# A recurrent attention with routed experts on Trainium2: score tile AB in two halves, two reads of a bank declared independent, capacity made a float elsewhere

## The chip, the cores and the metric

The kernel runs on one core of one Trainium2 chip. The metric is the device time of one execution in microseconds (us). A core has five engines with their own instruction queues: PE (TensorE, matrix products), DVE (VectorE), ACT (ScalarE), POOL (GpSimd) and SP (SyncE, which here only issues DMAs). They work side by side and wait for one another through semaphores. Matrix products are summed in banks of a memory of its own (PSUM, 128 partitions), from which ACT and DVE read. Tiles lie in SBUF, also over 128 partitions.

## The reference

Three stages follow one another. The first is a linear recurrence per batch and head (4 x 8 of them, 768 tokens, width 40):

```python
for t in range(S):
    y[:, :, t] = einsum('bhd,bhde->bhe', r_t, state)
    Sa = einsum('bhde,bhe->bhd', state, a_t)
    state = state * w_t[:, :, None, :] - einsum('bhd,bhe->bhde', Sa, b_t) + einsum('bhd,bhe->bhde', v_t, k_t)
```

Its output, 3072 tokens of width 320, is routed: each token goes to the expert with the largest logit, as the next row of that expert, as long as the expert has fewer than `capacity` rows (768, an input of the kernel). Each of the 8 experts computes `relu(x @ w1) @ w2` on its rows, times the gate. A last dense layer with ELU between two products (320 to 2048 to 320) runs on all 3072 tokens.

## The kernel before

**Attention** (`attention`, L76 to L673). The recurrence is computed in chunks of 64 tokens. A unit u (0 to 23) is one chunk of 16 of the 32 sequences, in two parts g. The order of all steps is written by hand, in the string `ORDER` (L33): a letter, the unit and the part, so `c8.1` is the next piece of the scores of unit 8, part 1. What follows is the order of instructions on each engine; no scheduler moves anything, and each engine goes through its own queue in order.

- `scores` (c, L229): four products on PE fill a PSUM bank "sc". ACT copies partitions 64 to 127 of it to the tile AB (L238). After part 1, SP sends AB to memory, as dab (L245, L248). There is one AB, in partitions 64 to 127, for all units: the copy of a unit waits until the DMA of the unit before has read it.
- `am_evac` (m, L250): DVE multiplies partitions 0 to 63 of the same bank by the mask and writes AM (L252). The framework takes the two reads of a bank, L238 and L252, as ordered: the second in the program waits for the first.
- `lm_load` (l, L287) loads dab back, row by row, for `solve` (i, L299 to L310), a triangular solve on POOL for a group of 2 or 4 units (`GROUPS`). Its result X goes out (dx, L316), and comes back as TT and TA (L336 to L342).
- `t64` (g, L379) puts the 64x64 inverse together from 32x32 blocks: DVE transposes a block of TA into T11 (L383), PE multiplies (xp, L390). T11 lies in the first 32 partitions of AB, which the scores don't use.
- `u_solve` (L426, L428), `vu_tr` (L436, L440), `s_update` (st, L451), `q_mm`, `y_mm` (Qs L487, y L509) carry the state on and make the output y, in RVU, VU, Qs, KB.
- `route` and `route_mm` (L526 to L564) choose the expert of each token and its row (roh, ACC, SLOT); `scatter` (L567) sends the rows to `disp`. `first` (F, L597) writes some index tiles on POOL, and `hot` (H, L583 to L593) prepares the first tokens of the experts with a one-hot product, pt.

**Experts and dense layer** (`ffn`). Weights are fetched by SP (L802, L804), split into a high part by ACT (L776) and a low part by POOL (L781). `marks` (L1259) runs first: on DVE it turns the capacity, an integer of two words (CAP), into a float (cf, four instructions L1262 to L1265); on POOL it sets some constants. Then `prep` (L944): ACT writes XH, the high part of the turned tokens (L953), DVE the rest, XL (L954), and `s1` (L969) multiplies the high and low weights by XH, then the high ones by XL, then both by XS (the last 64 rows). H and L (L1099, L1100) are the high and low parts of the hidden layer, po the second product (L1034 to L1042).

The lines of the attention and of `marks` that are touched:

Of the kernel before, what the change touches and what calls it, by code (L numbers as in the profile page):

```python
# [22 lines left out]
SL = 448  # L23
# [3 lines left out]
NU = 24  # L27
LOOK = 9

FU, KMU = 4, 8  # L30
GROUPS = [(u, 2) for u in range(0, FU, 2)] + [(u, 4) for u in range(FU, NU, 4)]

ORDER = """  # L33
# [42 lines left out]
def attention(tc, nc, e_in, v_tok, d_in, wg, disp, xt, cst, ring, early, early_w, cv, cap, after):  # L76
    ident, mask = cst["ident"], cst["mask"]
# [12 lines left out]
    sh = [ring.tile(i, F32) for i in (0, 1, 3)]  # L90
# [29 lines left out]
    XTs = [two.tile([128, 4, 128], F32, name="XT")]  # L120
    SD = [two.tile([128, 344], F32, name=f"SD{i}") for i in range(2)]
    AB = two.tile([128, 2, 4, 128], F32, name="AB")
    T11 = AB[:, 0].rearrange("p j (h t) -> p (j h) t", t=32).rearrange("p (b h) t -> p b h t", b=2)
    IW = two.tile([128, 4, 88], F32, name="IW")
    gap = two.tile([128, 1], F32, name="gap")
    st = {}
# [99 lines left out]
    def by_row(m):  # L226
        return m[:, 0:4096].rearrange("l (s t) -> s l t", t=64)

    def scores(u, g):  # L229
        A, kb = Abd[u % 2], KBt[u % 2]  # L230
        p = st["sc", u, g] = bank("sc")
        for i in range(4):
            q = 4 * g + i
            nc.tensor.matmul(  # L234
                p[:, 128 * i:128 * i + 128], kb[:, q].rearrange("p x t -> p (x t)"),
                A[:, :, q, :], start=True, stop=True)
        yield
        nc.scalar.copy(AB[64:128, :, 2 * g:2 * g + 2], p[64:128, :].rearrange("p (j b y) -> p b j y", j=2, b=2))  # L238
        if g == 0:
            return  # L240
        yield
        src = AB[64:128].rearrange("s b j (x t) -> s (b j x) t", t=64)
        if u < FU:
            st["dab", u] = dab = dr.tile([16, 4160], F32, name=f"dab{u}")
            nc.sync.dma_start(out=by_row(dab), in_=src)  # L245
        else:
            st["dab", u] = dab = dr.tile([64, 16, 64], F32, name=f"dab{u}")
            nc.sync.dma_start(out=dab, in_=src)  # L248

    def am_evac(u, g):  # L250
        AM, p = AMs[u % (LOOK + 1)], st["sc", u, g]
        nc.vector.tensor_tensor(  # L252
            AM[0:64, 4 * g:4 * g + 4].rearrange("p q x t -> p (q x) t"), p[0:64, :].rearrange("p (l t) -> p l t", t=64),
            mask[0:64].unsqueeze(1).to_broadcast([64, 8, 64]), op=ALU.mult)

    def kb_tr(u, g):
        kb, K = KBt[u % 2], KB[u % NKB]
# [121 lines left out]
    def t64(u):  # L379

        T, TA, TB = TT[u % 2], st["TA", u], TBs[u == 1]
        if u >= FU:
            nc.vector.transpose(out=T11[0:32].rearrange("p b h t -> p (b h t)"), in_=TA[64:96].rearrange("p b h t -> p (b h t)"))  # L383
            yield
        p = bank("xp")
        for h in range(8):
            for bp in range(2):
                r = slice(64 * bp, 64 * bp + 32)
                m, x = (st["M", u][r, h, 32:64], TB[r, h, 0]) if u < FU else (TA[0:32, bp, h], T11[0:32, bp, h])
                nc.tensor.matmul(p[64 * bp + 32:64 * bp + 64, 32 * h:32 * h + 32], m, x, start=True, stop=True)  # L390
# [223 lines left out]
    def warm(n):  # L614
        w = early_w.B[0]
        p = bank("warm")
        for _ in range(n):
# [4 lines left out]
                 b=route, j=route_mm, D=scatter, H=hot, F=first, W=lambda n, k: warm(n), Z=zero_d, X=zero_x, V=lambda: cv.pieces(spare, CVN))  # L622
# [60 lines left out]
def consts(p):  # L683

    c = {}
    c["ident"] = p.tile([128, 128], F32, name="ident")
    c["mask"] = p.tile([128, 64], F32, name="mask")
    for nm in ("ones", "tri"):
        c[nm] = p.tile([128, 128], BF, name=nm)
    c["desc"] = p.tile([128, 8], F32, name="desc")  # L690
    c["ebase"] = p.tile([128, 8], F32, name="ebase")
    c["lg"] = p.tile([128, 24, 9], F32, name="LG")
    c["oh"] = p.tile([128, 2, 8, 12], BF, name="OH")
    c["slot"] = p.tile([128, 24], I32, name="SLOT")
    c["acc"] = p.tile([128, 2, 8], BF, name="ACC")
    c["cap"] = p.tile([128, 2], I32, name="CAP")
    c["x"] = p.tile([128, 2048], F32, name="X0")
    c["xo"] = c["x"][:, 1536:1536 + RW]
    c["row"] = c["x"][:, 1536 + RW:1648 + RW]
    c["off"] = c["x"][:, 1648 + RW:1652 + RW]  # L700
    return c
# [185 lines left out]
def ffn(tc, nc, cst, disp, xt, w1, w2, w32, out, ring, W0, cv, ps, turned):  # L887
# [228 lines left out]
    def gates():  # L1116
# [3 lines left out]
        for nm in ("blk", "tmo", "l1"):  # L1120
# [19 lines left out]
        t = T("t", [128, 2, 8, 12])  # L1140
        nc.vector.tensor_tensor(t, p1.rearrange("p (b e c) -> p b e c", b=2, e=8),
                                b.unsqueeze(3).to_broadcast([128, 2, 8, 12]), op=ALU.add)
        nc.vector.scalar_tensor_tensor(out=t, in0=t, scalar=over["cap"], in1=OH, op0=ALU.is_lt, op1=ALU.mult)
        kp = T("kp", [128, 24])
        nc.vector.tensor_reduce(kp.rearrange("p (c b) -> p b c", b=2), t.rearrange("p b e c -> p b c e"), axis=AX.X, op=ALU.add)
        eb0 = T("eb0", [128, 8])
# [111 lines left out]

    def marks():  # L1259

        cw, cf = cst["cap"], ap.tile([128, 4], F32, name="cf", bufs=1)
        nc.vector.tensor_copy(cf[:, 0:2], cw)  # L1262
        nc.vector.tensor_scalar(cf[:, 2:3], cf[:, 0:1], 0.0, 4294967296.0, op0=ALU.is_lt, op1=ALU.mult)
        nc.vector.scalar_tensor_tensor(out=cf[:, 3:4], in0=cf[:, 1:2], scalar=4294967296.0, in1=cf[:, 2:3], op0=ALU.mult, op1=ALU.add)
        nc.vector.tensor_tensor(cf[:, 3:4], cf[:, 3:4], cf[:, 0:1], op=ALU.add)  # L1265
        over["cap"] = cf[:, 3:4]
        one = over["one"] = ap.tile([128, 8], F32, name="one", bufs=1)
        nc.gpsimd.memset(one, 1.0)
        start = over["start"] = ap.tile([128, 6], F32, name="begin", bufs=1)
        for i in range(4):  # L1270
            nc.gpsimd.iota(start[:, i:i + 1], pattern=[[0, 1]], base=112 * i, channel_multiplier=1, allow_small_or_imprecise_dtypes=True)
        nc.gpsimd.memset(start[:, 4:5], 0.0)
        nc.gpsimd.memset(start[:, 5:6], float(SL))
        cst["turn"] = ap.tile([128, 1], F32, name="turn", bufs=1)
        nc.gpsimd.memset(cst["turn"], 0.0)
# [82 lines left out]
    def counts():  # L1358

        p = ps.tile([128, 512], F32, tag="ph", name="pc")  # L1360
        nc.tensor.matmul(p[:, 0:8], cst["ones"], cst["acc"][:, 0], start=True, stop=True)
        yield
        cnt = over["cnt"] = ap.tile([128, 8], F32, name="cnt", bufs=1)
        nc.vector.tensor_copy(cnt, p[:, 0:8])
        cs, bi = ap.tile([128, 8], F32, name="cs", bufs=1), ap.tile([128, 8], I32, name="bi", bufs=1)
        nc.vector.tensor_tensor_scan(out=cs, data0=over["one"], data1=cnt, initial=0.0, op0=ALU.mult, op1=ALU.add)
        nc.vector.tensor_copy(bi, cs)
        yield
        rn = ap.tile([128, 4], F32, name="rn", bufs=1)
        ri = ap.tile([128, 1], I32, name="ri", bufs=1)  # L1370
        rg = ap.tile([128, 8], F32, name="rg", bufs=1)
        nc.vector.tensor_reduce(rn[:, 0:1], cnt, axis=AX.X, op=ALU.max)
        nc.vector.tensor_scalar(rn[:, 1:2], rn[:, 0:1], float(SL // 8), None, op0=ALU.add)
        nc.vector.tensor_scalar(rn[:, 2:3], over["cap"], float(SL), None, op0=ALU.min)
        nc.vector.tensor_tensor(rn[:, 2:3], rn[:, 0:1], rn[:, 2:3], op=ALU.is_gt)
        yield
        nc.vector.tensor_scalar(rg, cst["ebase"], 1.0 / 8, rn[:, 1:2], op0=ALU.mult, op1=ALU.is_lt)
        nc.vector.tensor_reduce(rn[:, 3:4], rg, axis=AX.X, op=ALU.add)
        nc.vector.tensor_scalar(ri, rn[:, 3:4], rn[:, 2:3], 1.0, op0=ALU.mult, op1=ALU.add)
        yield  # L1380
        _, over["base"] = nc.values_load_multi_w_load_instructions(bi[0:1, 0:7], (mybir.EngineType.SP,), min_val=0, max_val=NTOK)
        yield
        over["n"] = nc.values_load(ri[0:1, 0:1], min_val=1, max_val=8)
# [122 lines left out]
```

## Time and profile before

| | us |
|---|---|
| median of 3 runs | 1044.39 (1041.87 to 1047.43) |
| the profiled execution | 1040.54 |
| its span, first to last instruction | 1038.7 |

| engine | busy us | share of the span |
|---|---|---|
| PE | 950.6 | 92% |
| DVE | 738.3 | 71% |
| POOL | 617.1 | 59% |
| ACT | 516.6 | 50% |

The profile is one execution, recorded by the hardware; times are from its span's start. A timeline row gives start, busy time, engine, line, operation, tiles (out<-in), shapes and how many, and in brackets the idle time of the engine before it with what ended that. A row of waits gives who waited for whom, the total, the number of times and the longest. The attention lasts until about 437 us, the experts and the dense layer follow. The granted clock is the share of TensorE's full speed in a stretch: 1.00 is 2.4 GHz, 0.50 is 1.2 GHz, and values between are a mean of the two.

### The profile page before, as it was taken

How to read it: one execution, taken by the hardware profiler on the slowest of the kernel's cores; microseconds unless marked ns; L12 is line 12 of the kernel's file. 1: busy time of each engine (PE TensorE's matmuls, PEld its weight loads, DVE VectorE, ACT ScalarE, POOL GpSimd, SP SyncE). 2: the span in 40 equal slices, each digit the busy share in tenths (PEclk: the TensorE clock that was granted, in tenths of full speed). 3: DMA queues.
4: the chain of work that ended last, by engine and by line, in shares of the span. 5: the costliest groups of instructions: out<-in, count | busy, mean ns of one | idle time of the engine just before them, and what ended most of it. 6: DMA issues, size and time to landing. Idle time of an engine off the chain costs nothing.

```text
span 1038.7 us, 25351 instructions
## 1 busy us (share of the span) xinstructions
PE 950.6 (92%) x9994; PEld 860.9 (83%) x9994; DVE 738.3 (71%) x1291; ACT 516.6 (50%) x1013; POOL 617.1 (59%) x929
## 2 busy tenths in 40 slices
PE   4758989989899999789999999999999999999993
PEld 4758878888789888678889888888899888899993
DVE  8846848788675687658778877576766777677760
ACT  3636635666454434245544555565555555554550
POOL 4766979489898833467768787953333333333332
PEclk9967889999899999989999999999999999999997
DMA  6758875666565774646776866501010000100000
GB/s 161 174 159 173 182 162 120 144 139 145 127 120 119 171 195 99 170 141 203 214 236 201 250 186 217 187 23 26 27 27 26 11 28 13 27 26 1 26 2 28
DMA packets 181448, 121.69 MB, mean 117 GB/s; under 512 B 106256, under 2 KB 167336, under 8 KB 179688
## 3 DMA queue, kind: packets, MB, share of 16 engines
q1 hardware_dynamic: 175652, 99.63, 38.0%
q10 hardware_dynamic: 2500, 9.21, 3.4%
q0 software_dynamic: 3168, 11.14, 3.0%
q8 instruction: 81, 1.33, 0.5%
q14 instruction: 47, 0.39, 0.1%
HBM read 86.89 MB, written 33.05 MB: 115 GB/s over the span
## 4 chain that ended last, share of the span: by engine, by line
PE 54%; DVE 17%; DMA 16%; issue 5%; ACT 3%; POOL 3%; SPq 0%; ACTq 0%; DVEq 0%; POOLq 0%
PE ph L969 20%; DMA ring<-in_e_in_dram 5%; PE po L995 5%; PE po L996 5%; PE po L997 5%; DMA w<-E 4%; PE q L482 2%; PE sc L234 2%; DVE L L1100 1%; DVE ring L200 1%; PE x L519 1%; DVE E L860 1%; PE ut L426 1%; PE y L509 1%; DMA dab<-AB 1%
## 5 line engine op out<-in xcount | busy, mean ns | idle before, releaser
L781 POOL TENSOR_TENSOR ring<-ring,ring 128x64 fp32r<-128x64 f32 (+2 forms) x320 | 204.7, 675 | 72.4 <-ACT ring L776 72.4
L1114 POOL TENSOR_TENSOR L<-E,H 128x512 fp32r<-128x512 f32 x66 | 91.6, 1388 | 169.2 <-ACT H L1113 152.5
L969 PE MATMUL ph<-XH,ring 128*128 128x512 f32 (+1 forms) x640 | 169.9, 387 | 0.8 <-ACT XH L953 0.8
L1107 ACT ACTIVATE E<-N 128x512 f32<-128x512 f32 x96 | 60.7, 632 | 152.8 <-DVE N L1106 78.9
L310 POOL TENSOR_TENSOR X<-X,ring 128x60 f32<-128x60 f32 (+19 forms) x170 | 120.4, 708 | 13.3
L969 PEld LDWEIGHTS ph<-XH,ring 128*128 128x128 f32 x640 | 115.7, 190 | 14.9 <-ACT XH L953 1.4
L997 PE MATMUL po<-ring,L 128*128 128x320 f32 x384 | 119.4, 311 | 1.6 <-POOL L L1114 1.6
L995 PE MATMUL po<-ring,H 128*128 128x320 f32 x384 | 119.4, 311 | 0.2 <-ACT H L1113 0.2
L996 PE MATMUL po<-ring,H 128*128 128x320 f32 x384 | 119.2, 310 | 0.0
L969 PE MATMUL ph<-XL,ring 128*128 128x512 f32 (+1 forms) x320 | 97.9, 387 | 7.5 <-DVE XL L954 7.5
L969 PE MATMUL ph<-XS,ring 128*128 128x512 f32 (+1 forms) x320 | 96.9, 384 | 0.0
L1111 DVE SCALAR_TENSOR_TENSOR M<-E,M 128x512 f32<-128x512 f32 x96 | 78.0, 812 | 16.1 <-ACT M L1108 16.1
L1106 DVE TENSOR_SCALAR N<-ph 128x512 f32<-128x512 f32 x96 | 65.8, 685 | 27.7 <-PE ph L969 27.4
L308 POOL TENSOR_TENSOR ring<-X,ring 128x60 f32<-128x60 f32 (+19 forms) x108 | 65.0, 602 | 34.4 <-DMA ring<-dab 26.3
L995 PEld LDWEIGHTS po<-ring,H 128*128 128x128 f32 x384 | 72.8, 190 | 5.2 <-ACT H L1113 0.5
L996 PEld LDWEIGHTS po<-ring,H 128*128 128x128 f32 x384 | 72.7, 189 | 4.0
L969 PEld LDWEIGHTS ph<-XL,ring 128*128 128x128 f32 x320 | 60.7, 190 | 18.4 <-DVE XL L954 8.2
L997 PEld LDWEIGHTS po<-ring,L 128*128 128x128 f32 x384 | 72.7, 189 | 2.1 <-POOL L L1114 2.1
L1112 DVE SCALAR_TENSOR_TENSOR E<-ph,M 128x512 f32<-128x512 f32 x96 | 66.4, 692 | 8.1 <-DVE M L1111 0.5
L969 PEld LDWEIGHTS ph<-XS,ring 128*128 128x128 f32 x320 | 60.3, 189 | 11.2 <-DVE XS L954 0.4
L1100 DVE SCALAR_TENSOR_TENSOR L<-ph,H 128x448 fp32r<-128x448 f32 x64 | 39.4, 616 | 41.3 <-ACT H L1099 41.2
L1113 ACT CAST H<-E 128x512 fp32r<-128x512 f32 x96 | 59.0, 614 | 13.5 <-DVE E L1112 10.4
(261 smaller groups left out, 2176.5 us busy)
## 6 DMA issues: line engine op xcount, KB each, us to landing
ring<-in_w_dram SPq DMA_DIRECT2D x16, 640.0 KB
ring<-in_w_dram SPq DMA_DIRECT2D x32, 256.0 KB
dab<-AB SPq DMA_DIRECT2D x24, 256.0 KB
ring<-in_e_in_dram ACTq DMA_DIRECT2D x18, 321.6 KB
ring<-w SPq DMA_DIRECT2D x4, 1408.0 KB
disp<-ring SPq DMA_DIRECT2D x8, 575.8 KB
S<-in_w_out_dram SPq DMA_DIRECT2D x13, 320.0 KB
ring<-in_w_dram SPq DMA_DIRECT2D x32, 128.0 KB
```

Source lines behind the costliest of these rows:

```text
L308: nc.gpsimd.tensor_tensor(tv, X[:, 0:n, s:s + 1].to_broadcast([128, n, m]), N[:, s:s + 1, s + 1:e].to_broadcast([128, n, m]), op=ALU.mult)
L310: nc.gpsimd.tensor_tensor(X[:, 0:n, s + 1:e], X[:, 0:n, s + 1:e], tv, op=ALU.subtract)
L781: s.nc.gpsimd.tensor_tensor(B[:, to], r[:, q], B[:, q].bitcast(F32), op=ALU.subtract)
L969: nc.tensor.matmul(p, l, r[:, 0:s.T], start=i == 0, stop=i == len(seq) - 1)
L995: nc.tensor.matmul(o, H[:, c], hb, start=f == 0, stop=False)
L996: nc.tensor.matmul(o, H[:, c], lb, start=False, stop=False)
L997: nc.tensor.matmul(o, L[:, c], hb, start=False, stop=f == s.W.nf - 1)
L1106: nc.vector.tensor_scalar(N, p, 0.0, None, op0=ALU.min)
L1107: nc.scalar.activation(out=E, in_=N, func=AF.Exp)
L1111: nc.vector.scalar_tensor_tensor(out=M, in0=E, scalar=1.0, in1=M, op0=ALU.add, op1=ALU.mult)
L1112: nc.vector.scalar_tensor_tensor(out=E, in0=p, scalar=0.0, in1=M, op0=ALU.max, op1=ALU.add)
L1114: eng.tensor_tensor(L, E, H.bitcast(F32), op=ALU.subtract)
```

## The change

Three edits.

1. AB gets two halves: an even unit uses partitions 0 to 63, an odd one 64 to 127. So the copy of a unit waits for the DMA of the unit two back. T11, which had the first partitions of AB, goes to a stretch of the ring that TB of units under 4 used; from unit 16 (`LATE`) on, it is in AB again.
2. The copy L238 and the product L252 of a bank are declared independent (`apart`), so neither waits for the other.
3. The float capacity lies in a tile of the constants (CF), and its four DVE instructions move from `marks` to `first`, the step F near the end of the attention.

```diff
-FU, KMU = 4, 8
+FU, KMU, LATE = 4, 8, 16
...
-    T11 = AB[:, 0].rearrange("p j (h t) -> p (j h) t", t=32).rearrange("p (b h) t -> p b h t", b=2)
+    T11s = [x.rearrange("p (b h t) -> p b h t", b=2, t=32) for x in (sh[2][:, 2048:2560], AB[:, 0].rearrange("p j t -> p (j t)"))]
...
+    reads = {}
+
+    def apart(key, x):
+        if key in reads:
+            tc.declare_no_dep(x.ins, reads.pop(key), reason="partitions 0 to 63 and 64 to 127 of a bank are read apart")
+        else:
+            reads[key] = x.ins
+
     def scores(u, g):
...
-        nc.scalar.copy(AB[64:128, :, 2 * g:2 * g + 2], p[64:128, :].rearrange("p (j b y) -> p b j y", j=2, b=2))
+        lo = 64 * (u % 2)
+        apart(("sc", u, g), nc.scalar.copy(AB[lo:lo + 64, :, 2 * g:2 * g + 2], p[64:128, :].rearrange("p (j b y) -> p b j y", j=2, b=2)))
...
-        src = AB[64:128].rearrange("s b j (x t) -> s (b j x) t", t=64)
+        src = AB[lo:lo + 64].rearrange("s b j (x t) -> s (b j x) t", t=64)
...
     def am_evac(u, g):
         AM, p = AMs[u % (LOOK + 1)], st["sc", u, g]
-        nc.vector.tensor_tensor(
+        apart(("sc", u, g), nc.vector.tensor_tensor(
             AM[0:64, 4 * g:4 * g + 4].rearrange("p q x t -> p (q x) t"), p[0:64, :].rearrange("p (l t) -> p l t", t=64),
-            mask[0:64].unsqueeze(1).to_broadcast([64, 8, 64]), op=ALU.mult)
+            mask[0:64].unsqueeze(1).to_broadcast([64, 8, 64]), op=ALU.mult))
...
     def t64(u):
...
+        T11 = T11s[u >= LATE]
...
     def first():
+        cw, cf = cst["cap"], cst["cf"]
+        nc.vector.tensor_copy(cf[:, 0:2], cw)
+        nc.vector.tensor_scalar(cf[:, 2:3], cf[:, 0:1], 0.0, 4294967296.0, op0=ALU.is_lt, op1=ALU.mult)
+        nc.vector.scalar_tensor_tensor(out=cf[:, 3:4], in0=cf[:, 1:2], scalar=4294967296.0, in1=cf[:, 2:3], op0=ALU.mult, op1=ALU.add)
+        nc.vector.tensor_tensor(cf[:, 3:4], cf[:, 3:4], cf[:, 0:1], op=ALU.add)
...
-    c["cap"] = p.tile([128, 2], I32, name="CAP")
+    c["cap"], c["cf"] = p.tile([128, 2], I32, name="CAP"), p.tile([128, 4], F32, name="CF")
...
     def marks():
 
-        cw, cf = cst["cap"], ap.tile([128, 4], F32, name="cf", bufs=1)
-        nc.vector.tensor_copy(cf[:, 0:2], cw)
...
-        over["cap"] = cf[:, 3:4]
```

Two later lines read `cst["cf"][:, 3:4]` in place of `over["cap"]`.

On PE, ACT, POOL and SP the order of instructions is the same before and after; on DVE the four instructions of the capacity move. Line numbers of the changed kernel are higher by 9 or 10 in the attention and by 15 in `ffn`. The words in brackets of a row name what its instruction waits for: engines, and DMA lanes (DMAHW, DMASW).

DVE ahead of the first XL, before (L588 is the last step H of the attention):

```order
L564 TENSOR_TENSOR ACC<-ACC,roh 128x8
L587 TENSOR_TENSOR pos<-X_73,SLOT 128x4 [waits DVE_49]
L588 TENSOR_TENSOR hot<-X_73,pos 128x448 [waits DMAHW5_49,DVE_49]
L1262 CAST cf<-CAP 128x2 [waits DMAHW2_49,DMAHW1_49,DMAHW3_49,DMAHW0_49,DMAHW4_49,DMASW3_49,DMAHW5_49,DVE_49,DMAHW6_49,PE_49,DMAHW7_49,Activation_49,Pool_49]
L1263 TENSOR_SCALAR cf<-cf 128x1 [waits DVE_49]
L1264 SCALAR_TENSOR_TENSOR cf<-cf 128x1 [waits DVE_49]
L1265 TENSOR_TENSOR cf<-cf 128x1 [waits DVE_49]
L954 TENSOR_TENSOR XL<-pt,XH 128x448 [waits Activation_49] x2
L954 TENSOR_TENSOR XS<-pt,XS 64x448 [waits Activation_49]
```

And in the changed kernel:

```order
L572 COPY OH<-roh 128x8
L574 TENSOR_TENSOR ACC<-ACC,roh 128x8
L597 TENSOR_TENSOR pos<-X_74,SLOT 128x4 [waits DVE_49]
L598 TENSOR_TENSOR hot<-X_74,pos 128x448 [waits DMAHW5_49,DVE_49]
L969 TENSOR_TENSOR XL<-pt,XH 128x448 [waits DMAHW3_49,DMAHW4_49,DMAHW2_49,DMAHW5_49,DMAHW1_49,DMAHW6_49,DMAHW0_49,DMAHW7_49,DMASW3_49,Activation_49]
L969 TENSOR_TENSOR XL<-pt,XH 128x448 [waits Activation_49]
L969 TENSOR_TENSOR XS<-pt,XS 64x448 [waits Activation_49]
```

The four rows on cf are gone, and most of the waits of the first of them now stand on the first XL.

DVE at step F, before (L541 to L547 are the routing of the next-to-last tokens, L487 makes Qs for PE's y):

```order
L542 TENSOR_TENSOR req<-req,desc 128x8 [waits DVE_49]
L543 TENSOR_REDUCE rm_6291<-req 128x1 [waits DVE_49]
L544 TENSOR_TENSOR roh<-req,rm_6291 128x8 [waits DVE_49]
L547 TENSOR_TENSOR ACC<-ACC,roh 128x8 [waits DVE_49]
L487 TENSOR_TENSOR Qs<-q,mask 128x512
L487 TENSOR_TENSOR Qs<-q,mask 128x512 [waits PE_49]
L558 TENSOR_TENSOR rt<-rt,ebase 128x8 [waits PE_49]
L559 TENSOR_TENSOR rt<-rt,roh 128x8 [waits DVE_49]
```

And in the changed kernel:

```order
L552 TENSOR_TENSOR req<-req,desc 128x8 [waits DVE_49]
L553 TENSOR_REDUCE rm_6292<-req 128x1 [waits DVE_49]
L554 TENSOR_TENSOR roh<-req,rm_6292 128x8 [waits DVE_49]
L557 TENSOR_TENSOR ACC<-ACC,roh 128x8 [waits DVE_49]
L609 CAST CF<-CAP 128x2
L610 TENSOR_SCALAR CF<-CF 128x1 [waits DVE_49]
L611 SCALAR_TENSOR_TENSOR CF<-CF 128x1 [waits DVE_49]
L612 TENSOR_TENSOR CF<-CF 128x1 [waits DVE_49]
L497 TENSOR_TENSOR Qs<-q,mask 128x512
L497 TENSOR_TENSOR Qs<-q,mask 128x512 [waits PE_49]
L568 TENSOR_TENSOR rt<-rt,ebase 128x8 [waits PE_49]
```

The four rows now stand between ACC and the first Qs, without a wait for another engine.

ACT about the scores of unit 13 (the two copies to AB, and RVU, here under the name X, that PE's vu reads), before:

```order
L238 COPY AB<-sc 64x2x256 [waits DMAHW6_49,DVE_49,Activation_49]
L524 COPY XO<-x 128x320 [waits DMASW2_49]
L405 ACTIVATE TT_127<-t_2417 32x8x32 [waits PE_49]
L405 ACTIVATE TT_127<-t_2417 32x8x32
L238 COPY AB<-sc 64x2x256 [waits DVE_49,Activation_49]
L191 DMA VS_143<-in_v_tok_dram 64x640 [waits DMAHW4_49,DMAHW3_49]
L428 ACTIVATE X_73<-ut 128x8x64 [waits PE_49]
L265 COPY KB_118<-kbt 128x320 [waits PE_49] x2
L440 COPY VU<-vu 128x320 [waits PE_49,Activation_49]
L440 COPY VU<-vu 128x320 [waits PE_49]
```

And in the changed kernel:

```order
L247 COPY AB<-sc 64x2x256
L534 COPY XO<-x 128x320 [waits DMASW2_49]
L415 ACTIVATE TT_128<-t_2418 32x8x32 [waits PE_49]
L415 ACTIVATE TT_128<-t_2418 32x8x32
L247 COPY AB<-sc 64x2x256
L191 DMA VS_144<-in_v_tok_dram 64x640 [waits DMAHW4_49,DMAHW3_49]
L438 ACTIVATE X_74<-ut 128x8x64 [waits PE_49]
L274 COPY KB_119<-kbt 128x320 [waits PE_49] x2
L450 COPY VU<-vu 128x320 [waits PE_49,Activation_49]
L450 COPY VU<-vu 128x320 [waits PE_49]
```

The rows stand as they did; the two copies to AB have lost their waits for DVE, for the DMA lane and for ACT itself.

## Rows read from the trace of the kernel before

**Rows 1.** The longest waits of PE from 436 us to the end: total, times, longest.

```profile
PE ph L969 <- DVE XL L954: 7.5, 1, 7.5
PE po L997 <- POOL L L1114: 1.6, 2, 0.8
```

**Rows 2.** DVE timeline (start, busy, idle before), then all L954 (min/median/max ns).

```profile
436.85 8.24 DVE L1262 CAST cf<-CAP 128x2 f32<-128x2 int32 x1 [2.60 <-DMA ring<-in_w_dram]
445.12 0.15 DVE L1263 TENSOR_SCALAR cf<-cf 128x1 f32<-128x1 f32 x1
...
445.58 1.15 DVE L954 TENSOR_TENSOR XL<-pt,XH 128x448 fp32r<-128x448 f32 x2
...
L954 DVE TENSOR_TENSOR XL<-pt,XH x16: 607/616/625, 445.6 to 633.8; 128x448 fp32r<-128x448 f32 x16
```

**Rows 3.** POOL timeline beside it.

```profile
436.72 8.28 POOL L781 TENSOR_TENSOR ring<-ring,ring 128x64 fp32r<-128x64 f32 x16
```

**Rows 4.** PE timeline; then stretches with each engine's busy time and granted clock.

```profile
446.25 1.27 PE L969 MATMUL ph<-XL,ring 128*128 128x448 f32 x2 [7.54 <-DVE XL L954]
...
464.59 0.36 PE L1034 MATMUL po<-H,ring 128*128 128x448 f32 x1
...
445.00:448.00 3.00, 1.75 (x4) 1.10 (x5) 2.24 (x7) 0.52 (x1) 0.49 (x8) 0.50 0.57 165
448.00:451.00 3.00, 3.00 (x12) 2.51 (x11) 0.63 (x1) 0.54 (x1) 0.00 (x0) 0.63 0.89 234
```

**Rows 5.** Waits of ACT until 330 us; then durations of the copy and the product.

```profile
ACT AB L238 <- DVE AM L252: 23.9, 12, 4.1
...
ACT AB L238 <- DMA dab<-AB: 5.1, 3, 2.1
...
L238 ACT COPY AB<-sc x48: 562/581/582, 13.7 to 315.5; 64x512 f32<-64x512 f32 x48
...
L252 DVE TENSOR_TENSOR AM<-sc,mask x48: 644/673/683, 23.0 to 314.7; 64x512 f32<-64x512 f32 x48
```

**Rows 6.** Waits of PE from 100 to 320 us, its timeline, and one stretch's clock.

```profile
PE vu L436 <- ACT RVU L428: 4.0, 3, 1.7
...
PE st L451 <- ACT VU L440: 1.5, 2, 1.1
...
276.04 2.01 PE L234 MATMUL sc<-ring 128*128 128x128 f32 x8 [4.25 <-ACT ring L221]
...
302.54 0.93 PE L436 MATMUL vu<-ident,RVU 104*128 104x104 f32 x8 [1.67 <-ACT RVU L428]
...
300.00:320.00 20.00, 18.12 (x316) 16.95 (x316) 13.76 (x31) 11.09 (x24) 17.44 (x29) 0.91 0.46 102
```

**Rows 7.** ACT timeline early in the expert stage.

```profile
436.83 0.97 ACT L953 CAST XH<-pt 128x448 fp32r<-128x448 f32 x2 [2.56 <-PE pt L593]
...
460.06 0.78 ACT L776 CAST ring<-ring 128x704 fp32r<-128x704 f32 x1
460.74 0.53 ACT L1099 ACTIVATE H<-ph 128x448 fp32r<-128x448 f32 x1
```

**Rows 8.** Timelines of DVE, POOL and PE in step F and behind it.

```profile
424.47 1.52 DVE L544 TENSOR_TENSOR roh<-req,rm 128x8 bf16<-128x8 f32 x1
...
426.11 1.28 DVE L487 TENSOR_TENSOR Qs<-q,mask 128x512 f32<-128x512 f32 x2
...
431.63 0.89 POOL L584 TENSOR_TENSOR hot<-X,hot 128x321 fp32r<-128x321 f32 x1 [5.67 <-ACT hot L583]
...
426.84 1.28 PE L509 MATMUL y<-Qs,KB 128*64 128x64 f32 x32
```

**Rows 9.** SP timeline, and a step of the chain that ended last (start, us).

```profile
445.03 2.22 SPq L802 DMA_DIRECT2D ring<-in_w_dram  x4
...
430.40 6.46 DMA ring<-in_w_dram
```

**Rows 10.** POOL timeline at the start of the fifth solve.

```profile
208.39 0.68 POOL L308 TENSOR_TENSOR ring<-X,ring 128x31 f32<-128x31 f32 x1 [7.85 <-DMA ring<-dab]
```

More of the change, by code (lines that the diff above doesn't have):

```diff
@@ L1142, in gates @@
                                 b.unsqueeze(3).to_broadcast([128, 2, 8, 12]), op=ALU.add)
-        nc.vector.scalar_tensor_tensor(out=t, in0=t, scalar=over["cap"], in1=OH, op0=ALU.is_lt, op1=ALU.mult)
+        nc.vector.scalar_tensor_tensor(out=t, in0=t, scalar=cst["cf"][:, 3:4], in1=OH, op0=ALU.is_lt, op1=ALU.mult)
         kp = T("kp", [128, 24])
@@ L1259, in marks @@
     def marks():
-        cw, cf = cst["cap"], ap.tile([128, 4], F32, name="cf", bufs=1)
-        nc.vector.tensor_copy(cf[:, 0:2], cw)
-        nc.vector.tensor_scalar(cf[:, 2:3], cf[:, 0:1], 0.0, 4294967296.0, op0=ALU.is_lt, op1=ALU.mult)
-        nc.vector.scalar_tensor_tensor(out=cf[:, 3:4], in0=cf[:, 1:2], scalar=4294967296.0, in1=cf[:, 2:3], op0=ALU.mult, op1=ALU.add)
-        nc.vector.tensor_tensor(cf[:, 3:4], cf[:, 3:4], cf[:, 0:1], op=ALU.add)
-        over["cap"] = cf[:, 3:4]
         one = over["one"] = ap.tile([128, 8], F32, name="one", bufs=1)
@@ L1373, in counts @@
         nc.vector.tensor_scalar(rn[:, 1:2], rn[:, 0:1], float(SL // 8), None, op0=ALU.add)
-        nc.vector.tensor_scalar(rn[:, 2:3], over["cap"], float(SL), None, op0=ALU.min)
+        nc.vector.tensor_scalar(rn[:, 2:3], cst["cf"][:, 3:4], float(SL), None, op0=ALU.min)
         nc.vector.tensor_tensor(rn[:, 2:3], rn[:, 0:1], rn[:, 2:3], op=ALU.is_gt)
```

## The prediction

> **What bounds the kernel now.** The waits of TensorE (PE) were read first, from 436 us on, where the expert stages begin. PE stands still there almost nowhere: one wait of 7.5 us on XL, and the next in the list comes to 1.6 us in two pieces [rows 1]. So what is won before that wait, or in it, reaches the end nearly one for one. Next the DVE timeline beside that wait [rows 2]: the instruction ahead of XL is the CAST that turns the capacity into floats, 128x2 elements, and it takes 8.24 us, while its neighbour on 128x1 takes 0.15. The POOL timeline gives the reason: 16 subtractions L781 without a gap, from 436.72 for 8.28 us [rows 3]. The CAST starts 0.13 us behind the first of them and ends 0.1 us behind the last. XL itself (L954) takes 0.61 to 0.63 us in all its 16 cases [rows 2], so it is the CAST that is held, and XL only stands behind it. The PE row and the granted clock show what it costs: 7.54 us of idle time, then matmuls at 0.50 of full speed (1.2 of 2.4 GHz) until 448, and a mean of 0.63 in the 3 us behind [rows 4].
>
> For the score tile, the waits of ACT were read before 330 us: the copy to AB (L238) waits 23.9 us in 12 cases for DVE's masked product of the same bank, and 5.1 us in 3 for the DMA that reads AB [rows 5]. Only a part of this is passed on. PE's waits from 100 to 320 us that come right behind a held copy are those on RVU (4.0) and VU (1.5), 5.5 us together [rows 6].
>
> **The capacity.** Four DVE instructions leave the place ahead of XL. The release waits that hung on the CAST now hang on the first XL. They were over by 436.85, when the CAST began [rows 2]; XL needs XH, two casts that take 0.97 us together from 436.83 [rows 7], the first done near 437.3. So these waits cost nothing, by a margin of some 0.5 us. Two XL then run from 437.3 to 438.6, and PE ends its XH matmuls at 446.25 - 7.54 = 438.71 [rows 4]: the whole idle time goes, **-7.5 us**. If PE does not pause, it should not come to the lower clock either: (448 - 446.25) x (1 - 0.50) + 3 x (1 - 0.63) = **-2.0 us** [rows 4]. The pause is the only reason for the lower level that these rows show, so I take this in full, with 0 as the other bound.
>
> The four instructions go to step F, ahead of the products Qs at 426.11 [rows 8]. From the CAST's end at 445.09 to XL at 445.58 the other three cost 0.49 us [rows 2]; with 0.16 for a CAST that nothing holds, about their mean, the sum is **+0.65 us**. All of it is on the path: PE's y (L509) starts 0.1 us after the first Qs can be ready, and the routing of the last tokens follows from y. What could make it dearer is POOL. DVE's L544 just ahead took 1.52 us, to 425.99; POOL's next work is at 431.63, behind 5.67 idle us, and takes 0.89 us [rows 8]. Where the CAST now stands it has 5 us of free POOL; under such an instruction it would cost up to 0.9 more. Bounds 0.5 and 1.6; I take 0.65, because these rows have the CAST's new place in them.
>
> The rows also bear on how the sharing goes: 16 subtractions in a row kept the CAST out to the last [rows 2, 3]. The Trainium skill, SBUF — State Buffer, section "Who interferes with whom", says that DVE and GpSimd share one port pair, that a cast on DVE can need it, and that whoever issues first has it for that whole instruction. Read by the letter, the CAST would have got in after one of the 16 (0.52 us), some 7.7 us of it would be its own, and the total would be that of rival 2 below. The rows agree with the sharing, and show a hold over many instructions.
>
> **What is late next.** The second split of weights (L781, done at 445.0) is used by PE only after 454. But the fetch behind it starts when POOL is done, at 445.03 [rows 9], and that does not move against the end of the attention. A fetch of the same kind landed 6.46 us after its issue [rows 9], so its pieces, issued until 447.3, land near 453 to 454. ACT's cast that reads them stood at 460.06 [rows 7] and would come over 9 us sooner, at 451: ACT waits some 3 us. Behind it ACT has an activation H (460.74) [rows 7] that PE takes at 464.59 [rows 4], 3.85 us later. With 0.53 for H and 0.62 for the part that DVE makes of it, 2.7 us of this is slack. Between 0 and 2 us come back; I take **+0.8**.
>
> **AB in halves, reads apart.** Copy (0.58 us) and product (0.67 us) keep their times and engines [rows 5]; no instruction moves, only waits go. What limits the gain is the solve on POOL, paced by DMAs: POOL waited 7.85 us at 208.39 for the rows of a later unit [rows 10], and PE's largest wait of the middle part, 4.25 us for the ring at 276 [rows 6], comes out of that chain. What is won before 276 is swallowed there unless the chain itself starts sooner. The halves help here: a copy waits for the DMA of two units back, so the solve's input can leave earlier; but that DMA's issue on SP also stands behind other issues, so I give it a part. Lower end of the gain: only the RVU wait at 302.54, behind that point: 1.7 us. Upper end: all 5.5 us, and three stretches at the lower clock that follow such waits (160 to 180, 200 to 220 and 300 to 320 us each have a mean of 0.91, one shown in [rows 6]), at 20 x 0.09 = 1.8 us each: 11 us. On the bad side, a load that gets another DMA lane and is held there: a loss of 1.5, as the longest wait for AB's DMA came to about 2 [rows 5]. I take the 1.7 and half of the 4.0 + 1.5 - 1.7 = 3.8 us before 276: **-3.6 us**. T11 of the units before 16 goes to a place in the ring that only the first four units used, at no cost.
>
> **Sum.** -7.5 - 2.0 + 0.65 + 0.8 - 3.6 = -11.65 us. The profiled execution took 1040.54 us (span 1038.7 and 1.84 around it), 3.85 below the median of the three runs. On it the changed kernel comes to 1028.9; against the median 1044.39, by which I forecast, to **1032.7 us**.
>
> **Rivals.**
> 1. *The solve swallows all of the attention's gain*: the term -3.6 becomes 0, and the time 1036.3. For it: POOL's wait at 208.39 and PE's at 276 [rows 6, 10]; against it: the wait at 302.54 has no such point behind it.
> 2. *The CAST is slow by itself*, and only moves: 8.24 us in F, so Qs come 8.05 us later than in the forecast, PE waits there, and its clock may fall there (2.0): 1040.8 to 1042.8. Against it: the CAST ends within 0.1 us of POOL's row [rows 2, 3].
> 3. *More from the attention*: AB's DMAs leave earlier, the solve's chain follows, PE keeps its clock: -11 instead of -3.6, 1025.3.
> 4. *Much comes back behind 446*: ACT's wait for the fetch stops H and with it PE (+1.2 on the term), the clock falls there (+2.0), and the attention gives 0: 1039.5.
> 5. *Slower: the two reads of one bank stretch each other.* No row shows ACT and DVE reading one bank at once; the 48 pairs ran in turn. If each pair loses x on the path, the attention gives no gain and loses 48x: 1036.3 + 48x. It decides from x = 0.28 us (1049.7; a product of 0.95 instead of 0.67); 0.58, a whole copy, gives 1064. Against it: the two read different partitions, and most of the 48 are not on the path, by the 5.5 us that PE waited behind 29 us of held copies [rows 5, 6]. The Trainium skill, PSUM — Partial Sum Buffer, section "PSUM bank collisions raise a hardware error", has it that accesses to different quadrants (32 partitions) of a bank may go on at the same time, and that the hardware does not stall accesses that collide; by it x is 0. No row of the kernel before shows it.
>
> **How the numbers follow.** Forecast (1029 to 1036): 0.45. Rival 1 (1036 to 1038.5): 0.26. Rival 3: 0.13. Rival 4: 0.06. Rival 2: 0.06. Rival 5: 0.04. The range of 1024 to 1040 leaves out rivals 2 and 5 and some of 3. About 0.5% (5.2 us) is what a measurement of this kernel tells from no change. Under 1039.2 lie the forecast, rivals 1 and 3 and a part of 4: 0.86. Between 1039.2 and 1049.6 the rest of 4, and 2: 0.11. Above: 0.03.
>
> **What would show it.** In the changed profile: the CAST near 426 at 0.2 us or less, and Qs 0.6 to 0.7 us further behind the instruction ahead of the four; XL 0.1 us behind XH; no PE wait of over 0.2 us on XL; the clock at 1.00 over the first 15 us of the expert stage; AB waiting for no product; a wait of ACT's L776 about 14 us into that stage. Wrong would be: a CAST of several us in F, a PE wait on H of over 2 us early in the expert stage, copies or products well over 0.58 and 0.67 us, or, for rival 1, an attention that ends as late as before in spite of the missing waits.

## The result and the profile after

The changed kernel took 1032.8 us (median of 7 runs, 1030.6 to 1042.0), the kernel before 1044.4 beside it (7 runs, 1036.6 to 1047.4): a ratio of 0.9892, interval 0.9858 to 0.9926. All ratios, intervals and differences of means here leave out the few runs that were in a slower state. The forecast was 1032.7. The sum hit; its terms did not all, as the experiments show.

The first recorded execution was the longest of the seven, 1042.0 us. The rows below are from the second record of the same kernel, 1033.0 us. Lines of the changed kernel are 9 to 15 higher.

First the stretch about the start of the experts, DVE, POOL and ACT (start, busy time, engine, line, idle time before), then PE, and all waits of PE from 436 us to the end:

```profile
426.63 0.16 DVE L557 TENSOR_TENSOR ACC<-ACC,roh 128x8 bf16<-128x8 bf16 x1
426.72 0.16 DVE L609 CAST CF<-CAP 128x2 f32<-128x2 int32 x1
...
427.37 1.28 DVE L497 TENSOR_TENSOR Qs<-q,mask 128x512 f32<-128x512 f32 x2
...
438.66 1.16 DVE L969 TENSOR_TENSOR XL<-pt,XH 128x448 fp32r<-128x448 f32 x2 [3.12 <-ACT XH L968]
...
436.57 8.42 POOL L796 TENSOR_TENSOR ring<-ring,ring 128x64 fp32r<-128x64 f32 x16
...
438.10 0.97 ACT L968 CAST XH<-pt 128x448 fp32r<-128x448 f32 x2 [2.57 <-POOL ring L796]
...
454.09 0.78 ACT L791 CAST ring<-ring 128x704 fp32r<-128x704 f32 x1
```

```profile
439.83 0.57 PE L984 MATMUL ph<-XL,ring 128*128 128x448 f32 x2
...
PE po L1012 <- POOL L L1129: 1.5, 2, 0.8
PE ph L984 <- ACT XH L968: 0.8, 1, 0.8
PE po L1010 <- ACT H L1128: 0.2, 1, 0.2
```

The CAST takes 0.16 us in F; ahead of XL it took 8.24 [rows 2]. From ACC to Qs it is now 0.74 us; before, 0.08 (ACC at 426.03, Qs at 426.11 [rows 8]). XL starts 0.56 us behind the first XH cast (438.10), while POOL is in the midst of its 16 subtractions, which run as long as before [rows 3], and PE reads it without a wait. The 7.5 us at the head of the list in [rows 1] are gone. The granted clock, in stretches of 3 us (the column after POOL's busy time and count), does not fall there any more, against 0.50 and 0.63 in [rows 4]:

```profile
438.00:441.00 3.00, 2.20 (x8) 1.51 (x9) 1.77 (x3) 1.88 (x4) 3.00 (x7) 1.00 0.49 187
441.00:444.00 3.00, 3.00 (x16) 2.60 (x16) 1.18 (x2) 1.12 (x3) 3.00 (x7) 1.00 0.33 65
444.00:447.00 3.00, 3.00 (x16) 2.76 (x15) 0.72 (x6) 0.38 (x2) 1.48 (x10) 1.00 0.59 185
```

Then the score tile: ACT's waits before 330 us, the durations of copy and product (minimum, median, maximum in ns), and PE's longest waits from 100 to 320 us.

```profile
ACT AB L247 <- PE sc L242: 5.6, 7, 2.4
ACT AB L247 <- DMA ring<-dab: 2.6, 1, 2.6
...
L247 ACT COPY AB<-sc x48: 561/582/582, 13.4 to 313.7; 64x512 f32<-64x512 f32 x48
...
L261 DVE TENSOR_TENSOR AM<-sc,mask x48: 644/673/684, 23.5 to 313.2; 64x512 f32<-64x512 f32 x48
```

```profile
PE x L529 <- DVE XT L523: 3.6, 3, 2.2
PE sc L242 <- ACT ring L221: 3.3, 2, 2.7
PE xp L400 <- DVE ring L393: 2.5, 2, 1.9
```

All 23.9 us of waits on the product and the 5.1 on AB's own DMA [rows 5] are gone, and of PE's 5.5 us on RVU and VU [rows 6] 0.2 are left in those rows. But PE has other waits in their place, and this kernel's attention is not shorter: its first XH cast stands at 438.1, at 447.7 in the first record, and at 436.83 before [rows 7]. What lies behind that cast is shorter: 593.1 and 592.6 us, against 1038.7 - 436.8 = 601.9.

### The profile page after: what moved, and what is told of

Read it like the earlier page. It is cut to its first block, busy times and chain, and to the rows that moved or that the text cites. A ratio compares the mean times of both kernels' runs of the same rounds, so it can differ in the third digit from the quotient of the medians.

```text
span 1040.3 us, 25344 instructions
## 1 busy us (share of the span) xinstructions
PE 963.1 (93%) x9994; PEld 870.7 (84%) x9994; DVE 730.1 (70%) x1291; ACT 517.7 (50%) x1013; POOL 617.2 (59%) x929
## 4 chain that ended last, share of the span: by engine, by line
PE 64%; DVE 14%; DMA 8%; issue 5%; POOL 3%; ACT 3%; SPq 1%; POOLq 0%; DVEq 0%; ACTq 0%; another core or an unknown queue 0%
PE ph L984 20%; PE po L1010 5%; PE po L1012 5%; PE po L1011 5%; PE q L492 4%; PE sc L242 3%; DMA ring<-in_e_in_dram 2%; PE ut L436 2%; PE x L529 2%; DMA w<-E 2%; PE y L519 2%; PE y L506 2%; PE st L461 2%; PE rhs L426 1%; DVE L L1115 1%
## 5 line engine op out<-in xcount | busy, mean ns | idle before, releaser
L319 POOL TENSOR_TENSOR X<-X,ring 128x60 f32<-128x60 f32 (+19 forms) x170 | 109.4, 644 | 13.3
L317 POOL TENSOR_TENSOR ring<-X,ring 128x60 f32<-128x60 f32 (+19 forms) x108 | 74.1, 686 | 32.8 <-DMA ring<-dab 24.7
```

The source lines that it names most:

```text
L317: nc.gpsimd.tensor_tensor(tv, X[:, 0:n, s:s + 1].to_broadcast([128, n, m]), N[:, s:s + 1, s + 1:e].to_broadcast([128, n, m]), op=ALU.mult)
L319: nc.gpsimd.tensor_tensor(X[:, 0:n, s + 1:e], X[:, 0:n, s + 1:e], tv, op=ALU.subtract)
```

## Experiments

Theory A is the forecast: about 8 us from the capacity, 3.6 from the edits on AB. Theory B gives all of the gain to the capacity. Single runs of one kernel lie up to 12.5 us from its median, so each kernel of the table was run 6 to 12 times, beside the kernel before. A ratio is not the quotient of the two medians beside it, which for the third series of the changed kernel would be 0.9956. Where a difference in us stands behind a ratio, it is the ratio's distance from 1 times the median of the kernel before.

| kernel | runs | median us | before us | ratio | interval |
|---|---|---|---|---|---|
| all, first | 7 | 1032.8 | 1044.4 | 0.9892 | 0.9858 to 0.9926 |
| all, second (r1) | 7 | 1032.0 | 1040.8 | 0.9890 | 0.9851 to 0.9930 |
| all, third (r10) | 12 | 1037.5 | 1042.1 | 0.9933 | 0.9903 to 0.9963 |
| capacity in F alone (r2) | 6 | 1027.2 | 1040.8 | 0.9884 | 0.9844 to 0.9923 |
| the same again (r9) | 12 | 1033.8 | 1042.1 | 0.9923 | 0.9885 to 0.9962 |
| capacity near 55 us alone (r8) | 7 | 1034.7 | 1044.2 | 0.9895 | 0.9857 to 0.9933 |
| the same again (r11) | 6 | 1032.8 | 1042.1 | 0.9893 | 0.9853 to 0.9932 |
| all, capacity near 55 us (r12) | 6 | 1030.5 | 1042.1 | 0.9879 | 0.9842 to 0.9916 |
| AB in halves and reads apart (r3) | 12 | 1038.4 | 1040.8 | 0.9982 | 0.9950 to 1.0014 |
| halves alone (r5) | 12 | 1042.6 | 1044.2 | 0.9976 | 0.9942 to 1.0009 |
| apart alone (r6) | 12 | 1040.6 | 1044.2 | 0.9989 | 0.9950 to 1.0028 |
| all, CAST again ahead of XL (r4) | 10 | 1038.5 | 1040.8 | 0.9995 | 0.9958 to 1.0031 |

### All once more

No edit.

> The changed kernel once more, for a profile beside its median. Of its seven runs the profiled one took 1042.0 us, the others 1030.6 to 1033.8, and in that profile the attention lasts 11 us longer than in the profile of before. Theory A (the edits hold what the forecast said: 9 us of the gain behind the attention, 3.6 in it): the typical run takes 1032 to 1034, the first XH cast stands at 433 to 438 us, and the rest after it is 9 us shorter than the 601.9 us of before. Theory B (the edits make the attention longer, and the 11.6 us come from the rest alone): XH at 440 or later in a run near the median, and a rest over 12 us shorter than before.

Measured: median 1032.0; in the recorded run XH at 438.1 and 593.1 us behind it, 8.8 less than before. Theory A holds for the part behind the attention. For the attention neither came in this record: it is as long as before, though theory A had it 3 us shorter. In the record of the third series (r10), which is near its median, XH stands at 443.4, as theory B had it, but the 592.6 us behind it are 9.3 less than before and not over 12.

### The capacity alone

```diff
     def first():
+        (the four instructions on cst["cf"])
...
     def marks():
-        (the four instructions on cf)
```

> The kernel before with the capacity's four instructions moved alone. Theory A: -7.5 - 2.0 + 0.65 + 0.8 = -8.0 us, a ratio of 0.992, about 1036 beside 1044; no PE wait on XL, the CAST 0.16 us in F. Theory B (all of the change's gain is the capacity's): -11.6, a ratio of 0.989.

Measured: 0.9884, -12.1 us with an interval of -16.2 to -8.0. That is theory B's number, with A's just at the interval's end. The repetition below gave 0.9923, -8.0. In both records PE has no wait on XL, and the CAST takes 0.16 us in F.

### AB and the reads alone

The changed kernel with the four instructions back in `marks`:

```diff
     def first():
-        (the four instructions on cst["cf"])
...
     def marks():
+        (the four instructions on cf)
```

> The changed kernel with the capacity where it was: AB in halves and the reads apart alone. Theory A: -3.6 us, a ratio of 0.9965, the PE wait on XL of 7.5 us as before and no wait of AB on the product. Theory B (the solve swallows it): 0 to +1 us, a ratio of 1.000 or just over, with PE's waits on RVU and VU gone but its waits at the solve's results larger by as much.

Measured: 0.9982, -1.9 us (-5.2 to +1.5). The interval holds both theories. That the capacity's move alone removes PE's wait on XL, the records of the kernel above show; here, with the edits on AB alone, it is there again:

```profile
PE ph L979 <- DVE XL L964: 6.1, 1, 6.1
```

### The CAST again, and a reduction in front of it

The changed kernel and two more instructions, whose results nobody reads:

```diff
     def marks():
+        again = ap.tile([128, 4], F32, name="again", bufs=1)
+        nc.vector.tensor_reduce(again[:, 2:3], cst["cf"][:, 0:2], axis=AX.X, op=ALU.max)
+        nc.vector.tensor_copy(again[:, 0:2], cst["cap"])
```

> The changed kernel with two more DVE instructions in front of XL: a TENSOR_REDUCE (one small tile read) and then the CAST of the capacity as it was, into a tile that nobody reads. Theory A (POOL keeps the CAST out, whatever the CAST): the CAST takes about 8 us and ends within 0.2 us of POOL's 16 subtractions, the reduction in front of it 0.2 us; 8 to 9 us of the gain go, 1041 to 1042. Theory B (the CAST is slow only the first time or by itself, not by POOL): 0.2 us or a length unrelated to POOL's end; and 1033. If the reduction is held too, it is not the kind of instruction that matters.

Measured: 0.9995, so nearly all of the gain is gone. DVE and POOL in its record:

```profile
439.39 0.15 DVE L1277 TENSOR_REDUCE again<-CF 128x1 f32<-128x2 f32 x1 [2.45 <-POOL ring L796]
439.46 6.79 DVE L1278 CAST again<-CAP 128x2 f32<-128x2 int32 x1
445.48 1.14 DVE L969 TENSOR_TENSOR XL<-pt,XH 128x448 fp32r<-128x448 f32 x2
...
437.83 8.31 POOL L796 TENSOR_TENSOR ring<-ring,ring 128x64 fp32r<-128x64 f32 x16
...
PE ph L984 <- DVE XL L969: 5.1, 1, 5.1
```

The CAST began 1.6 us behind POOL's first subtraction this time and its record ends at 446.25, 0.11 behind POOL's last (446.14). XL starts already at 445.48, which is 6.1 us behind the first XH cast (439.37) instead of 0.56, and PE waits 5.1 us for it. In the three other records with the CAST in its old place it took 6.65 (r3), 7.93 (r5) and 7.93 us (r6) and ended 0.53 us ahead of the end of POOL's string, 0.03 behind it and 0.03 behind it: where the CAST ends goes with POOL, whenever it begins. The CAST in F took 0.16 us in the same execution, at 428.0. So it is POOL that holds it, and rival 2 (slow by itself) falls. The reduction, at the same place and under the same subtractions, takes 0.15 us: the kind of instruction matters.

### A sum of two tiny tiles in the CAST's place

```diff
     def marks():
+        again = ap.tile([128, 4], F32, name="again", bufs=1)
+        nc.vector.tensor_tensor(again[:, 0:1], cst["cf"][:, 0:1], cst["cf"][:, 1:2], op=ALU.add)
```

> The changed kernel with one more DVE instruction in front of XL: a TENSOR_TENSOR of two tiny tiles in SBUF, 128x1 each, into a tile that nobody reads. Theory A (what needs the shared port waits, whatever its size): it starts behind POOL's first subtraction and is held for about 8 us, as the CAST was, and 8 to 9 us of the gain go. Theory B (only the CAST, or only the first instruction that changes the type): 0.2 us, and the gain stays.

Measured: one run, 1031.9 us, too little to say what it costs in all. The record says what it does:

```profile
434.28 6.00 DVE L1277 TENSOR_TENSOR again<-CF 128x1 f32<-128x1 f32 x1 [2.61 <-PE pt L603]
...
432.54 8.31 POOL L796 TENSOR_TENSOR ring<-ring,ring 128x64 fp32r<-128x64 f32 x16
...
PE ph L984 <- DVE XL L969: 4.7, 1, 4.7
```

A sum over 128x1 is held for 6.0 us and ends at 440.28, about where POOL's last subtraction begins (440.85 less one sixteenth of 8.31). So it is not the change of type that POOL keeps out: an instruction that reads two tiles in SBUF is kept out too, and XL, which reads one tile in SBUF and one bank, is not.

### Halves alone, reads apart alone

The two edits on the attention, each by itself, the capacity as before. Without `apart`:

```diff
-        apart(("sc", u, g), nc.scalar.copy(AB[lo:lo + 64, ...], p[64:128, :]...))
+        nc.scalar.copy(AB[lo:lo + 64, ...], p[64:128, :]...)
...
-        apart(("sc", u, g), nc.vector.tensor_tensor(AM[0:64, ...], ...))
+        nc.vector.tensor_tensor(AM[0:64, ...], ...)
```

> The kernel before with AB in halves alone; the two reads of a bank stay in order, the capacity stays where it was. Theory A (the halves let the solve's input leave earlier): -1 to -2 us, ACT's waits of 5.1 us for the DMA gone. Theory C (formed on the first four runs: waits go, but what PE wins it gives back at the next wait or at the lower clock): within 3 us of before, PE's idle time in the attention within 2 us of the 59.9 us of before.

Measured: 0.9976, -2.5 us (-6.1 to +0.9). ACT's waits for AB's own DMA are gone, as theory A had it. PE's idle time is 55.9 us in the record, 4.0 less than before, twice what theory C allowed.

And without the halves, with one AB and T11 in its old place:

```diff
-        lo = 64 * (u % 2)
-        apart(("sc", u, g), nc.scalar.copy(AB[lo:lo + 64, ...], p[64:128, :]...))
+        apart(("sc", u, g), nc.scalar.copy(AB[64:128, ...], p[64:128, :]...))
```

> The kernel before with the two reads of a bank declared independent alone; one AB, the capacity where it was. Theory A: ACT's 23.9 us of waits on the product go, PE's waits on RVU and VU (5.5 us) with them, -2 to -4 us. Theory C: PE's idle time in the attention falls from 59.9 us by 2 to 3, its time at the lower clock (75 us before) does not fall, and the total stays within 3 us. Theory D (two reads of one bank at once stretch each other): copies over 0.60 us or products over 0.70.

Measured: 0.9989, -1.1 us (-5.2 to +2.9). ACT's waits on the product and PE's on RVU and VU are gone, as theory A had it; PE's idle time, 58.0 us, and its time at the lower clock, 82.1, are about as theory C had them. Neither edit alone can be told from nothing. The medians of 582 and 673 ns say little on theory D, which is rival 5: of the 48 pairs of copy and product only 7 overlap in the second record of the changed kernel, taken pair by pair in the order of the queues. It falls by these 7, with copies of 562 to 582 ns and products of 673 to 684, within 1 ns of the ranges of [rows 5]. Four of them start at the same moment, as here (ACT, then DVE):

```profile
226.52 0.58 ACT L247 COPY AB<-sc 64x512 f32<-64x512 f32 x1 [0.33 <-PE sc L242]
...
226.52 0.68 DVE L261 TENSOR_TENSOR AM<-sc,mask 64x512 f32<-64x512 f32 x1 [1.04 <-PE sc L242]
```

### The capacity early

The kernel before, with the four instructions ahead of the first transpose of the solve (`t32`), near 55 us:

```diff
     def t32(u):
...
+        if "cap" not in st:
+            st["cap"] = True
+            (the four instructions on cst["cf"])
         turn()
```

> The kernel before with the capacity's four instructions moved to the first part of the attention, near 55 us, where DVE was idle for 7.5 us, and nothing else changed. Theory A: the same gain behind the attention as with step F, and the 0.65 us in F saved: -8.7 to -10 us, 0.65 less than the kernel with the capacity alone moved to F, which a measurement cannot tell apart; the distance from ACC to Qs in F is back at 0.08 us. It goes wrong if POOL is busy at 55 us: then the CAST is held there, in front of the transpose that waits for the solve.

Measured: 0.9895, -11.0 us (-14.9 to -7.0). Qs (426.14) stand 0.08 us behind ACC (426.06) again. At 55 us the CAST took 0.52 us (DVE, then POOL):

```profile
55.08 0.52 DVE L357 CAST CF<-CAP 128x2 f32<-128x2 int32 x1
...
54.58 0.99 POOL L299 MEMSET XB<- 128x1040 f32 x1
```

POOL was busy there, which is what the expectation named as going wrong: the CAST ended at 55.60, 0.03 us behind a memset of POOL. It cost nothing, because DVE waited another 3.85 us for the solve behind the four instructions.

### Two pairs on one chip

What the edits on AB are worth on top of the capacity: the capacity in F (r9) and near 55 us (r11), and the same with them (r10, the changed kernel, and r12, the changed kernel with the four instructions taken from `first` to `t32` as above).

> The capacity alone in F, a second time, beside the three that follow. The four are two pairs, without and with the edits on AB and its reads. Theory A (those edits are worth 3.6 us): this one near -8 us against before, the pair with the edits 3 to 4 us shorter. Theory C (PE's idle time in the attention falls by some 4 us with the edits, its time at the lower clock grows, and the two cancel): -8 to -12 us here, and the pair with the edits within 3 us of it or longer. In the profile: idle 58 to 62 us up to the first XH cast, 68 to 76 us at the lower clock.

> The changed kernel, a third time. Theory A: 3 to 4 us shorter than the capacity alone in F. Theory C: within 3 us of it or longer; in the profile 55 to 58 us idle in the attention, 80 to 105 us at the lower clock.

> The capacity alone, near 55 us, a second time. 0.65 us under the capacity in F by both theories, not to be told apart from it by the time; profile as that one: 58 to 62 us idle, 68 to 76 us at the lower clock.

> The changed kernel with the capacity's four instructions near 55 us instead of step F. Theory A: the best of the four, -12.3 us against before. Theory C: as the changed kernel less 0.65 us; 54 to 57 us idle, 80 to 105 us at the lower clock; within 3 us of the capacity alone near 55 us, or longer.

Measured, against the same kernel before: 0.9923 without and 0.9933 with them in F, 0.9893 without and 0.9879 with them near 55 us. One pair is +1.0 us, the other -1.5, each uncertain by 4 us or more, too much to exclude theory A's 3.6. In means of runs there are four such comparisons, each on one chip: +2.1 us (r1 less r2), +0.5 (r10 less r9), -0.6 (r12 less r11) and -1.3 (r3 less the kernel before). Weighted by their scatter they give -0.2, with an interval of about -2 to +2. Theory A's 3.6 us are not there; a smaller gain or loss cannot be excluded. For r12 alone theory A was right: it is the best of the four, -12.6 where -12.3 was expected, but its partner without the edits on AB is at -11.2.

The records show how a kernel with fewer waits comes out no shorter. One row each for the stretch from the start to the first XH cast: its length, PE's busy time, and after POOL's busy time the mean granted clock. In this order: before, capacity alone (r9), all twice (r1, r10).

```profile
0.00:436.80 436.80, 376.87 (x6957) 347.39 (x6957) 315.93 (x623) 217.03 (x475) 304.35 (x504) 0.91 0.66 151
```

```profile
0.00:438.40 438.40, 372.82 (x6957) 342.22 (x6957) 317.57 (x627) 216.89 (x476) 305.21 (x506) 0.93 0.64 151
```

```profile
0.00:438.10 438.10, 380.76 (x6957) 350.81 (x6957) 316.16 (x627) 216.61 (x475) 308.47 (x507) 0.90 0.65 150
```

```profile
0.00:443.40 443.40, 386.00 (x6957) 354.48 (x6957) 314.61 (x627) 217.46 (x475) 308.27 (x506) 0.90 0.64 148
```

The length less PE's busy time is its idle time: 59.9 and 65.6 us without the edits on AB, 57.3 and 57.4 with them. The same number of matmuls (6957) takes longer with them, at a lower mean clock. Time at the lower level is twice the sum of (1 - clock) x length, here over slices of 5 us. All records together (us):

| edits on AB | record | attention | PE idle | at the lower clock | behind it |
|---|---|---|---|---|---|
| none | before | 436.8 | 59.9 | 75.4 | 601.9 |
| none | r2 | 431.1 | 58.2 | 68.4 | 591.1 |
| none | r9 | 438.4 | 65.6 | 61.4 | 592.5 |
| none | r8 | 436.9 | 62.4 | 75.1 | 590.0 |
| none | r11 | 440.3 | 64.6 | 75.2 | 589.5 |
| halves | r5 | 440.1 | 55.9 | 88.6 | 600.2 |
| apart | r6 | 435.9 | 58.0 | 82.1 | 599.2 |
| both | all, first | 447.7 | 57.1 | 105.8 | 592.6 |
| both | r1 | 438.1 | 57.3 | 85.3 | 593.1 |
| both | r10 | 443.4 | 57.4 | 88.7 | 592.6 |
| both | r12 | 439.6 | 59.9 | 81.9 | 593.7 |
| both | r3 | 427.7 | 54.9 | 75.2 | 599.1 |
| both | r4 | 439.4 | 56.2 | 99.0 | 600.4 |
| both | r7 | 434.3 | 54.8 | 82.0 | 595.8 |

With both edits PE's idle time is 56.8 us in the mean, without them 62.1: 5.3 us are won. The time at the lower clock is 88.3 us against 71.1; the work done in the 17.2 us more would take half as long at full clock, so 8.6 us are lost. That makes +3.3; the mean lengths, 438.6 and 436.7, differ by +1.9, which single records with a spread of 3 to 6 us cannot tell from nothing. The direction is theory C's; its ranges were missed by the idle time of r9, r11 and r12 and by the time at the lower clock of r9. The two groups hardly overlap: the least idle time without the edits is 58.2 us (r2) and the most with both 59.9 (r12), the most time at the lower clock without them 75.4 (before) and the least with both 75.2 (r3). Part of the two shifts can be one and the same: a PE at the lower clock takes longer over its own work and so may wait less for the others.

One place can be named. In the kernel before PE waits between 207 and 212 us three times, for 1.12, 1.13 and 0.32 us, and then has both Qs for y ready. In seven of the eight records with the reads apart (all but r1) PE comes to y sooner and there waits for the second Qs, 2.0 to 2.4 us in one piece: in DVE's queue it stands behind the product AM and two more (L210, L212), which take about as long as before. PE and its clock, before and in the first record of the changed kernel:

```profile
210.12 0.67 PE L451 MATMUL st<-VU,KB 128*64 128x40 f32 x16 [1.13 <-ACT VU L440]
...
200.00:220.00 20.00, 16.32 (x275) 14.50 (x275) 15.91 (x34) 11.06 (x23) 10.84 (x19) 0.91 0.49 114
```

```profile
210.64 1.12 PE L519 MATMUL y<-Qs,KB 128*64 128x64 f32 x16 [2.41 <-DVE Qs L497]
...
200.00:220.00 20.00, 16.39 (x214) 14.78 (x211) 16.27 (x32) 9.83 (x21) 14.08 (x21) 0.75 0.59 125
```

From 200 to 225 us the seven records have 6.8 to 15.2 us at the lower clock; r1, where no wait there is longer than 0.95 us, has none, and the records without `apart` have at most 3.4. The means of the two groups of the table differ here by 6.4 us, of the 17.2 in all. That the longer wait brings the clock down fits these records; no experiment took it away, and where the rest comes from stays open.

## Why the forecast held, and where it did not

**The wait on XL, -7.5.** Right in mechanism and size. Behind the first XH cast the eight records of kernels without anything ahead of XL have 589.5 to 593.7 us, mean 591.9; the four records with the CAST in its old place (before, r3, r5, r6) 599.1 to 601.9, mean 600.1. That is 8.2 us less, where -7.5 - 2.0 + 0.8 = -8.7 was forecast.

**The clock behind it, -2.0.** It came: 1.00 in all three stretches above, against 0.50 and 0.63 [rows 4].

**The fetch that is late next, +0.8.** It did not come. ACT's cast of that fetch stands 16.0 us behind XH in the second record (454.09), not 14; ACT came to it later by its own work, and PE has no wait on H of over 0.2 us. Within the noise of these means the term is 0 to 0.8.

**The capacity in F, +0.65.** Right: 0.74 us from ACC to Qs instead of 0.08.

**The edits on AB, -3.6.** This step failed. Over the four comparisons they measured -0.2 us, about -2 to +2. The step counted PE's waits behind held copies (5.5 us) as time that reaches the end, and in its upper end gave them the clock as a gain as well. The waits did go, but PE took part of them up again as one longer wait on DVE's Qs, and its time at the lower clock, for which the step allowed no loss, grew by 17.2 us, a loss of 8.6 against the 5.3 us of idle time won. That the clock falls because of such waits is argued from the records and not shown by an experiment.

**Rival 1** gave the right amount, a term of 0, but the records do not bear out its reason: nothing shows the solve swallowing the gain. POOL's wait of 7.85 us for the solve's input [rows 10] was shorter in the first record of the changed kernel, as its waits from 190 to 215 us show, and is absent in the second:

```profile
POOL ring L317 <- DMA ring<-dab: 4.8, 1, 4.8
```

and PE's wait on ACT's ring, 4.25 us [rows 6], is 2.7 at most in the second. **Rival 2** fell by the CAST in F and by the CAST again ahead of XL (its 8.05 us would be 8.24 - 0.16 = 8.08); **rival 3** by the four comparisons; **rival 4** by the clock and PE's waits behind 438 us; **rival 5** by the seven pairs that overlap.

**The sum.** The first measurement agrees with the forecast within 0.1 us; that is luck. In the three series of the changed kernel the mean is 9.5, 8.7 and 6.4 us below that of the kernel before beside it, weighted 7.8 with a standard error of 1.0, where 11.65 was forecast. The capacity's share, forecast at -8.0, measured -9.2 (standard error 0.8) in the four series of its own kernels. The -3.6 that is missing lies inside what a single series of seven runs cannot tell.

No kernel here beats the others beyond the intervals. The capacity near 55 us has the same effect as in F without its 0.66 us; with the edits on AB it had the lowest ratio, 0.9879 (0.9842 to 0.9916), and the capacity alone gave 0.9893 and 0.9895.

## What to carry to other kernels

A tiny instruction with a long duration can be a wait in disguise: look at what the neighbouring engine does from its first to its last moment, and move it to where that engine rests, instead of making it faster. Waits that are taken off an engine which is not the bound need not shorten the kernel: here PE's idle time fell and the time did not. The next wait of the bound engine and its granted clock have to be in the account before a gain is counted. Where single runs spread by ten microseconds, a change of three takes a pair of kernels on one chip, several times.

## What the runs showed of the hardware

That the CAST was held through all of POOL's string, and not for one subtraction of 0.52 us, was new to me in the rows before, and it came again: 6.79 us, and 6.0 for a sum of two tiles of 128x1, each from its start to within about one subtraction of the end of POOL's string. A reduction of one such tile took 0.15 us in the same place, and XL, from a bank and a tile, between 0.61 and 0.63 in all its 16 cases, two of them under the string. Near 55 us the CAST took 0.52 us in one record (r8), 1.48 in another (r11) and 1.77 in a third (r12), and ended each time 0.03 us behind the end of a memset of POOL, so a memset, which reads no tile, held it too:

```profile
L366 DVE CAST CF<-CAP x1: 1774/1774/1774, 53.0 to 53.0; 128x2 f32<-128x2 int32 x1
```

In the seven pairs that overlap, ACT and DVE read the two halves of one bank at the same time without either taking longer than before (copies up to 582 ns, products up to 684). And the same program's attention can differ by 10 us between two executions (438.1 and 447.7), with the granted clock as the visible difference: 85 against 106 us at the lower level.
